# Two changes to a fused attention and expert kernel: three 32-row copies for four 19-row copies, and two key units scored later

## The chip, the cores and the metric

The kernel runs on one core of a Trainium2 chip. The metric is the device time of one execution in microseconds (us); lower is better. Times before: a median of 1031.72 us of three runs (1028.29 to 1032.41).

## The reference

Agent attention over four batches, then a mixture of experts in which each token takes its best expert. Cut to what matters:

```python
B, N, C = 4, 11456, 128;  n_agents = 49;  E, F = 8, 1024
a2k = softmax(scale * agents @ k.T)            # 49 x N per batch
agent_v = a2k @ v                              # 49 x C
q2a = softmax(scale * q @ agents.T)            # N x 49
x = q2a @ agent_v                              # N x C, all tokens 45824 x C
e_idx = argmax(x @ w_gate)
probs, eom = softmax(x @ w_gate), sigmoid(x @ w_output_gate)
h = relu(x @ w1[e]);  out = probs[e] * eom[e] * (h @ w2[e])     # e = e_idx of the token
```

Everything is float32; the kernel splits most factors into a high and a low half in float16.

## The kernel before, in words

Tokens are cut per batch into 12 units: 11 of 1024 tokens (128 partitions by 8) and one of 192 (96 by 2). Each unit of queries gives two tiles of the main products (512 tokens, or one tile of 192), 92 tiles in all.

*Why x need not be formed.* A token's hidden value is relu(e @ (agent_v @ w1)), with e the 49 exponentials of the token. `fold(b)` therefore takes the average values of a batch, picks the one expert that most of its tokens are expected to take (`ei`), loads that expert's `w1t` and `w2t`, and multiplies the first with agent_v (`products`, results `aw`). `first` makes the float16 weights `w` of it. Each half of the 1024 hidden values needs two `w`: one (`rest`) with low parts for the rest of the agents, repeated in four groups of rows, and one (`own_`) of 128 rows: the 49 high weights, the same 49 for the low half of e, and 30 low weights for the high half of e. The 30 low rows and the 19 of `rest` together are all 49 agents. Tokens whose expert is another one are done apart at the end ("left" tiles).

*Turned queries.* `q_rest` makes for each query unit the exponentials `ef`, their high and low half in `e16` (49 + 49 columns, and 30 columns of the high half again, 128 in all), and turns `e16` by a DMA transpose into `x1` (128 rows of 1024 float16 values). Four copies from `x1` into the row groups of a second tile, `x2`, follow; each waits for the transpose. Both tiles are called `x_ld` in the profile. Then the logits (`lg`) are taken from `x1`, and the expert of each token, its factor `smt`, and what the left tiles need (`efd`) follow.

*Main products.* `mm1` multiplies four blocks of `own_` with `x1` and four blocks of `rest` with the four row groups of `x2`, into four PSUM banks (`h`). ACT makes `hh` of it (relu, float16), DVE `hl` (what is left of it), and `mm2` multiplies both with the second weights `vv` into `y`.

*Order.* All instructions are emitted by one program that plays a schedule with its own estimates: `Clock` holds for each engine and tile when it thinks it is free or ready. `main_stream` emits `mm1` and `mm2` when their operands are ready by these estimates; between them `tick` lets other streams go on. While nothing is ready before the main products begin, `idle` emits `warm` products of constants. `clk.started` becomes true with the first `mm1`. Every engine executes in order.

One stream, `small_products`, scores keys, queries and values in the order of `ITEMS`: 12 key units of batch 0, two query units, 12 value units, six key units of batch 1 (`PRE = 6`), then query units mixed with the keys and values of the next batch. A query unit waits until it is at most `AHEAD = 5` units ahead of the main products. `scores` has two forms for whole float32 units: before the start single products of 64 columns each, after it a block of products of 32 columns (`blocked`). `loads` loads the units in the same order; the first `FIRST_ITEMS = 2 * NU + 6` (30) at once, the rest after the weights that `fold` picks. In a unit's float32 products each matmul shows as two records.

All DMAs named here are issued by SP, whose queue is in order too. In the profile nearly all instructions have line L212, that of the helper that emits them, so groups are told apart by their tiles.

Of the kernel before, what the change touches and what calls it, by code (L numbers as in the profile page):

```python
# [17 lines left out]
P = 128  # L18
B, N, C, A, E, F = 4, 11456, 128, 49, 8, 1024
# [14 lines left out]
AD = P - 2 * A  # L34
AR = A - AD
G4 = 4
# [225 lines left out]
def agent_attention_top1_moe(ctx, tc, qT, kT, v, aT, wg, wo, w1, w2, cst, out):  # L262
    nc = tc.nc
    clk = Clock()
    ACT, DVE, POOL = Engine(clk, "ACT", nc.scalar), Engine(clk, "DVE", nc.vector), Engine(clk, "POOL", nc.gpsimd)
    PE, SY = Engine(clk, "PE", nc.tensor), Engine(clk, "SP", nc.sync)
# [42 lines left out]
    def release(k):  # L309
        banks[k][0] = True  # L310
# [143 lines left out]
    halves = {}  # L454
# [119 lines left out]
    parts = {}  # L574
# [44 lines left out]
    def loads():  # L619
        for n, item in enumerate(ITEMS):  # L620
            while n >= FIRST_ITEMS and (picking[0] or len(X1) < 2):
                yield None
# [6 lines left out]
    def scores(item, name):  # L629

        kind, b, u = item
        base, pp, nt = UNITS[u]
        whole = item in WHOLE
        while item not in (parts if whole else halves):
            yield None
        yield from wait_free(True)
        if whole:
            x, inv = parts.pop(item), None
            todo = [(x, at)]
        else:  # L640
            xh, xl, inv = halves.pop(item)
            todo = [(xh, ah), (xh, al), (xl, ah)]
        s = bank(name)
        mark = hold(True)
        if whole and clk.started:
            yield from blocked(s, [(t, x[:, t * pp:(t + 1) * pp], at[:, b, :]) for t in range(nt)])
            scored(item)
            return s, mark, inv
        for t in range(nt):
            if whole and pp == P:  # L650

                for h in range(0, P, 64):
                    yield from PE.q.matmul(s[h:h + 64, t * A2:(t + 1) * A2], x[:, t * pp + h:t * pp + h + 64],
                                           at[:, b, :], start=True, stop=True)
                continue
            for k, (x, a) in enumerate(todo):
                yield from PE.q.matmul(s[0:pp, t * A2:(t + 1) * A2], x[:, t * pp:(t + 1) * pp], a[:, b, :],
                                       start=(k == 0), stop=(k == len(todo) - 1))
        scored(item)
        if not whole:  # L660
            scored_n[0] += 1
        return s, mark, inv

    NU = len(UNITS)
# [162 lines left out]
    def fold(b):  # L827

        ad, ar = avd[b % 2]
        while "rec" not in K[b]:  # L830
            yield None
        av = K[b]["av"]
        yield from DVE.q.tensor_tensor(ad[:, 0:A], av[:, 0:A], K[b]["rec"][:, 0:A], op=ALU.mult)
        if b == 0:
            release(K[0]["mark"])
        sa = wk.tile([P, 1], F32, name=f"sa{b}", tag="sa")
        yield from DVE.q.tensor_reduce(sa, ad[:, 0:A], axis=AX.X, op=ALU.add)
        wgs = wk.tile([P, E], F32, name=f"wgs{b}", tag="wgs")
        yield from DVE.q.tensor_scalar(wgs, wgo[:, 0:E], sa, None, op0=ALU.mult)
        yield from wait_free()  # L840
        ga = bank(f"ga{b}")
        mark = hold()
        yield from PE.q.matmul(ga[:, 0:E], ones, wgs, start=True, stop=True)
        yield from ACT.q.copy(ad[:, A:2 * A], ad[:, 0:A])
        yield from ACT.q.copy(ad[:, 2 * A:P], ad[:, 0:AD])
        yield from POOL.q.tensor_copy(ar[:, :, 0:AR], ad[:, AD:A].unsqueeze(1).broadcast_to([P, G4, AR]))
        gm1 = wk.tile([P, 2], F32, name=f"gm1{b}", tag="gm1")
        yield from DVE.q.tensor_reduce(gm1[:, 0:1], ga[:, 0:E], axis=AX.X, op=ALU.max)
        r1 = wk.tile([P, E], F32, name=f"r1{b}", tag="r1")
        yield from DVE.q.scalar_tensor_tensor(r1, ga[:, 0:E], gm1[:, 0:1], rank8, op0=ALU.is_ge, op1=ALU.mult)  # L850
        release(mark)
        yield from DVE.q.tensor_reduce(gm1[:, 1:2], r1, axis=AX.X, op=ALU.max)
        ei = wk.tile([P, 1], I32, name=f"ei{b}", tag="ei")
        yield from DVE.q.tensor_scalar(ei, gm1[:, 1:2], -1.0, float(E), op0=ALU.mult, op1=ALU.add)
        picking[0] = True
        state[b] = dict(w=[], vv=[])
        spawn(gates(b, ad), -1)
        yield from SY.wait(ei)
        er = nc.values_load(ei[0:1, 0:1], engines=[SP], min_val=0, max_val=E - 1,
                            skip_runtime_bounds_check_because="eight minus a rank of one to eight")  # L860
        w1t = wk.tile([P, F], F32, name=f"w1t{b}", tag="w1t", bufs=2)
        for hf in range(2):
            sl = slice(hf * 512, (hf + 1) * 512)
            yield from SY.q.dma_start(w1t[:, sl], w1[bass.ds(er, 1), :, sl].rearrange("a p f -> p (a f)"))
        w2t = wk.tile([P, F], F32, name=f"w2t{b}", tag="w2t", bufs=2)
        yield from SY.q.dma_start(w2t, w2[bass.ds(er, 1)].rearrange("a p f -> p (a f)"))
        spawn(picked(w2t), -1)
        aw, marks = [], []
        spawn(products(b, ad, ar, w1t, aw, marks), -1)
        ndom = wk.tile([P, E], F32, name=f"ndom{b}", tag="ndom")  # L870
        yield from DVE.q.tensor_scalar(ndom, rank8, gm1[:, 1:2], None, op0=ALU.not_equal)
        state[b]["ndom"] = ndom
        sq = wk.tile([P, 2], F32, name=f"sq{b}", tag="sq")
        for hf in range(2):
            x = wk.tile([P, 512], F16, name=f"wsq{b}_{hf}", tag="whi", bufs=2)
            yield from ACT.q.activation(x, w1t[:, hf * 512:(hf + 1) * 512], AF.Square, accum_out=sq[:, hf:hf + 1])
        while "an" not in state[b]:
            yield None
        r, mark = yield from total(sq, f"mw{b}")
        c1 = wk.tile([P, 1], F32, name=f"c1{b}", tag="c3")  # L880
        yield from DVE.q.tensor_scalar(c1, r, state[b]["an"], None, op0=ALU.mult)
        release(mark)
        s1, s1i = yield from scale(c1, f"s1{b}", 10)
        state[b]["s1i"] = s1i
        spawn(first(b, aw, marks, s1), -1)
        spawn(second(b, w2t), -1)

        yield from wait_free()
        t = bank(f"avn{b}")
        mark = hold()  # L890
        yield from PE.q.transpose(t[0:A, 0:P], ad[:, 0:A], idf)
        avn = wk.tile([P, C], F32, name=f"avn_sb{b}", tag="avn", bufs=1)
        yield from ACT.q.copy(avn[0:A], t[0:A, 0:P])
        release(mark)
        yield from SY.q.dma_start(avnd[b], avn[0:A])
# [120 lines left out]
    def q_rest(b, u, s, mark, inv):  # L1016
        base, pp, nt = UNITS[u]
# [12 lines left out]
        ev = ef[0:pp, 0:nt, 0:A]  # L1030
        yield from ACT.q.activation(ev, z[0:pp, 0:nt, 0:A], AF.Exp,
                                    scale=SCALE if inv is None else inv[0:pp])
        e16 = e16s[(NU * b + u) % 4]
        yield from ACT.q.copy(e16[0:pp, 0:nt, 0:A], ev)
        yield from LOW.q.tensor_tensor(e16[0:pp, 0:nt, A:2 * A], ev, e16[0:pp, 0:nt, 0:A], op=ALU.subtract)
        yield from POOL.q.tensor_copy(e16[0:pp, 0:nt, 2 * A:P], ev[:, :, 0:AD])
        while me > 0 and rests[me - 1] < 1:
            yield None
        while vacant_turned() is None:
# [1 line left out]
        x1 = place(("x1", b, u), vacant_turned()[1], [1024], F16)  # L1041
# [2 lines left out]
        while vacant_turned() is None:  # L1044
            yield None
        x2 = place(("x2", b, u), vacant_turned()[1], [1024], F16)
        for g in range(G4):
            yield from SY.q.dma_start(x2[32 * g:32 * g + AR, 0:nt * pp], x1[AD:A, 0:nt * pp])
        X1[b, u] = x1, x2
        rests[me] = 1  # L1050
        while not {"gs", "ndom"} <= state.get(b, {}).keys() or (me > 0 and rests[me - 1] < 2):
# [110 lines left out]
    MIX = [(3, 0)] * 4 + [(0, 0)] + [(0, 2)] * 6 + [(0, 0)]  # L1162
    ITEMS = order()
    UNIT = {"q": q_unit, "k": k_unit, "v": v_unit}
    FIRST_ITEMS = 2 * NU + 6

    WHOLE = {x for x in ITEMS if x[0] == "k" or x[1] == 0 and x[2] < 8 or x[1] == B - 1}

# [19 lines left out]
    def mm1(i, hf):  # L1188

        b, u, h, pp, n = tiles[i]  # L1190
        w = pp * n
        own_, rest = state[b]["w"][hf]
        x1, x2 = (x[:, 512 * h:512 * h + w] for x in X1[b, u])
        p = []
        for g in range(G4):
            p.append((bank(f"h{i}_{hf}_{g}", k=g), hold()))
            PE.matmul(p[g][0][:, 0:w], own_[:, g * P:(g + 1) * P], x1, start=True, stop=False)
            if g < G4 - 1:
                tick()
        for g in range(G4):  # L1200
            rows = slice(32 * g, 32 * g + AR)
            PE.matmul(p[g][0][:, 0:w], rest[rows, g * P:(g + 1) * P], x2[rows, :], start=False, stop=True)
        for g in range(G4):
            spawn(relu(i, G4 * hf + g, *p[g]), 0)
        tick(0)
        block()
        if hf == 1 and 4 * h + n == UNITS[u][2]:
            for x in ("x1", "x2"):
                scored((x, b, u))
        tick(0)  # L1210
# [546 lines left out]
```

## Time and profile before

| | |
|---|---|
| median of three runs | 1031.72 us (1028.29 to 1032.41) |
| the profiled execution | 1036.13 us |
| its span, first to last instruction | 1034.4 us |
| PE, PEld busy | 971.5 us (94%), 738.6 us (71%) |
| DVE, ACT, POOL busy | 803.7 us (78%), 669.6 us (65%), 429.6 us (42%) |
| mean granted TensorE clock | 0.983 |
| DMA | 146.68 MB, mean 142 GB/s |
| copies from x1 to x2 (`x_ld<-x_ld`) | 192, 38.0 KB each (7.1 KB for the small units) |
| transposes (`x_ld<-e`) | 48 |

A row of a timeline has the start in us, the duration in us, the engine, the line, the operation with what it writes and reads, how many instructions are merged in it, and in brackets how long the engine was idle before it and what ended that. SPq is SP's queue. A row of the waits has the total in us, how many times, and the longest. A row of stretches has, for each engine (PE, PEld, DVE, ACT, POOL), busy us and instructions, then the granted clock, the busy share of the DMA engines and GB/s.

### The profile page before, as it was taken

Reading aid. Unit: us, or ns where it says so; the run is one execution under the profiler, and the core shown is the slowest. Engines: PE = TensorE matmul, PEld = TensorE weight load, DVE = VectorE, ACT = ScalarE, POOL = GpSimd, SP = SyncE. Lnnn points to the kernel's source line nnn. Section 1 sums busy time; section 2 is a strip of 40 time slices with the busy share of each in tenths; the row PEclk is TensorE's granted clock in tenths of the full one; section 3 lists DMA queues with packets and bytes.
Section 4 is the critical chain, followed back from the end, with each engine's and each line's share of the span. In section 5 each row is a group of like instructions: output and inputs, shape, how many; then the busy total and the mean of one; then the engine's idle time right before and its main releaser. Section 6 shows DMA issues by size and latency. Waiting matters only on the chain. (4 is left out here: it accounts for less than half of the span.)

```text
span 1034.4 us, 36058 instructions
## 1 busy us (share of the span) xinstructions
PE 971.5 (94%) x14800; PEld 738.6 (71%) x14800; DVE 803.7 (78%) x2167; ACT 669.6 (65%) x1523; POOL 429.6 (42%) x722
## 2 busy tenths in 40 slices
PE   9879988999999899999999999999998999999985
PEld 8666666777687677776677677776765777888764
DVE  2738877878888778888988878888997876766662
ACT  3336856787778787778688886657554665555542
POOL 1403445564244476453345556522243354442121
PEclk9989999999999999999999999999999999999998
DMA  8975745653556746545377454444342344545020
GB/s 317 273 241 153 149 106 102 160 156 113 169 150 195 159 110 123 160 129 177 93 184 192 124 153 139 144 127 126 97 94 80 107 157 132 153 150 151 23 76 27
DMA packets 106396, 146.68 MB, mean 142 GB/s; under 512 B 60466, under 2 KB 69094, under 8 KB 106228
## 3 DMA queue, kind: packets, MB, share of 16 engines
q1 hardware_dynamic: 104884, 142.86, 49.7%
q8 instruction: 117, 1.92, 0.8%
q0 software_dynamic: 1344, 1.49, 0.7%
q14 instruction: 51, 0.42, 0.1%
HBM read 90.88 MB, written 35.17 MB: 122 GB/s over the span
## 5 line engine op out<-in xcount | busy, mean ns | idle before, releaser
L212 PE MATMUL y<-vv,hh 128*128 128x256 f16 (+1 forms) x2880 | 546.6, 275 | 16.4 <-DVE os L212 7.3
L212 DVE SCALAR_TENSOR_TENSOR hl<-h,hh 128x512 f16<-128x512 f32 (+1 forms) x736 | 448.8, 667 | 92.0 <-ACT hh L212 86.3
L212 PE MATMUL y<-vv,hl 128*128 128x128 f16 (+1 forms) x2880 | 513.5, 220 | 4.7 <-DVE hl L212 3.8
L212 ACT ACTIVATE hh<-h 128x512 f16<-128x512 f32 (+1 forms) x736 | 373.4, 592 | 196.0 <-PE h L212 194.1
L212 PEld LDWEIGHTS <-hh 128*128 128x128 f16 (+1 forms) x2880 | 284.2, 99 | 57.4 <-issue 22.3
L212 PEld LDWEIGHTS <-hl 128*128 128x128 f16 (+1 forms) x2880 | 285.1, 100 | 25.0 <-issue 14.7
L212 PE MATMUL h<-x_ld,w 128*128 128x512 f16 (+1 forms) x1472 | 260.8, 377 | 4.6 <-DVE hl L212 4.0
L212 PEld LDWEIGHTS <-w 128*128 128x128 f16 x1472 | 83.1, 94 | 108.5 <-issue 77.0
L212 POOL TENSOR_TENSOR os<-os,smt 128x512 f32<-128x512 f32 (+1 forms) x92 | 96.2, 1046 | 117.3 <-DVE os L212 94.6
L212 DVE TENSOR_TENSOR os<-y,ys 128x256 f32<-128x256 f32 x180 | 74.9, 416 | 42.6 <-ACT ys L212 39.9
L212 ACT COPY ys<-y 128x256 f32<-128x256 f32 x180 | 68.6, 381 | 53.0 <-PE y L212 47.7
L212 POOL TENSOR_TENSOR e<-ef,e 128x392 f16<-128x392 f32 (+1 forms) x48 | 42.3, 881 | 63.5 <-ACT e L212 63.4
L212 POOL TENSOR_TENSOR q_ld<-q_ld,xhq 128x1024 f16<-128x1024 f32 (+1 forms) x28 | 55.0, 1965 | 28.0 <-ACT q_ld L212 27.5
L212 POOL TENSOR_TENSOR ev<-S,km_o 128x400 f32<-128x400 f32 (+1 forms) x44 | 42.2, 961 | 42.1 <-PE av L212 38.0
L212 PE MATMUL ks<-at,k_ld 128*32 128x50 f32 (+1 forms) x2280 | 48.9, 216 | 7.9 <-DMA k_ld<-kT 5.7
L212 PEld LDWEIGHTS ks<-at,k_ld 128*32 128x32 f32 (+1 forms) x2280 | 41.9, 119 | 17.8 <-issue 14.7
L212 PE MATMUL lh<-lxs,lw_ld 128*128 128x128 f32 x224 | 43.4, 275 | 0.8 <-ACT lxs L212 0.8
L212 PE MATMUL ly<-lw_ld,lh 128*128 128x128 f32 x224 | 43.2, 275 | 0.0
L212 PEld LDWEIGHTS <-xhq 128*128 128x128 f16 (+1 forms) x412 | 33.5, 97 | 10.3 <-issue 4.1
L212 PE MATMUL lg<-gs,x_ld 128*128 128x36 f16 x360 | 33.9, 181 | 6.1 <-DMA x_ld<-e 4.9
L212 POOL TENSOR_TENSOR ll<-lL,rr 128x128 f32<-128x128 f32 (+1 forms) x48 | 19.1, 398 | 48.8 <-DVE rr L212 46.9
L212 PEld LDWEIGHTS <-x_ld 128*128 128x128 f16 x360 | 27.2, 99 | 16.3 <-DMA x_ld<-e 7.2
(273 smaller groups left out, 1313.7 us busy)
## 6 DMA issues: line engine op xcount, KB each, us to landing
q_ld<-qT SPq DMA_DIRECT2D x44, 512.0 KB
v_ld<-v SPq DMA_DIRECT2D x44, 512.0 KB
out<-os SPq DMA_DIRECT2D x88, 256.0 KB
k_ld<-kT SPq DMA_DIRECT2D x43, 512.0 KB
lw_ld<-w SPq DMA_DIRECT2D x28, 512.0 KB
efd<-ef SPq DMA_DIRECT2D x44, 200.0 KB
x_ld<-x_ld SPq DMA_DIRECT2D x176, 38.0 KB
w1t<-w SPq DMA_DIRECT2D x8, 256.0 KB
```

Of the source, the lines that this page charges most:

```text
L212: return getattr(self.eng, op)(*a, **k)
```

## The change

The 30 agents whose low weights stand in the 128-row product are now the last 30 instead of the first 30, and the 19 in groups the first 19. Rows 0 to 18 of `x1` are these 19 agents, and they already lie where group 0 reads them. So group 0 reads `x1` itself, and three copies fill the groups 1 to 3 of `x2`; each takes 32 rows of `x1` instead of 19. Apart from that, the key units 4 and 5 of batch 1 wait in `scores` until the main products have begun, and with them all that follows them in `small_products`. `FIRST_ITEMS` is written in another way and keeps its value, 30.

```diff
@@ scores
-        while item not in (parts if whole else halves):
+        while item not in (parts if whole else halves) or kind == "k" and b == 1 and u >= EARLY and not clk.started:
             yield None
@@ fold
         yield from ACT.q.copy(ad[:, A:2 * A], ad[:, 0:A])
-        yield from ACT.q.copy(ad[:, 2 * A:P], ad[:, 0:AD])
-        yield from POOL.q.tensor_copy(ar[:, :, 0:AR], ad[:, AD:A].unsqueeze(1).broadcast_to([P, G4, AR]))
+        yield from ACT.q.copy(ad[:, 2 * A:P], ad[:, AR:A])
+        yield from POOL.q.tensor_copy(ar[:, :, 0:AR], ad[:, 0:AR].unsqueeze(1).broadcast_to([P, G4, AR]))
@@ q_rest
-        yield from POOL.q.tensor_copy(e16[0:pp, 0:nt, 2 * A:P], ev[:, :, 0:AD])
+        yield from POOL.q.tensor_copy(e16[0:pp, 0:nt, 2 * A:P], ev[:, :, AR:A])
...
-        for g in range(G4):
-            yield from SY.q.dma_start(x2[32 * g:32 * g + AR, 0:nt * pp], x1[AD:A, 0:nt * pp])
+        for g in range(1, G4):
+            yield from SY.q.dma_start(x2[32 * g:32 * g + 32, 0:nt * pp], x1[0:32, 0:nt * pp])
@@
-    FIRST_ITEMS = 2 * NU + 6
+    EARLY = 4
+    FIRST_ITEMS = 2 * NU + 2 + EARLY
@@ mm1
-            PE.matmul(p[g][0][:, 0:w], rest[rows, g * P:(g + 1) * P], x2[rows, :], start=False, stop=True)
+            PE.matmul(p[g][0][:, 0:w], rest[rows, g * P:(g + 1) * P], (x2 if g else x1)[rows, :], start=False, stop=True)
```

With A = 49, P = 128: AD = 30, AR = 19, G4 = 4, NU = 12.

## The prediction

> **What bounds the kernel now.** I read first the page's busy times, then the stretches, to see where TensorE stands still, then its waits, then the timeline around the largest one.
>
> ```profile
> PE 971.5 (94%) x14800; PEld 738.6 (71%) x14800; DVE 803.7 (78%) x2167; ACT 669.6 (65%) x1523; POOL 429.6 (42%) x722
> ```
>
> ```profile
> 50.00:75.00 25.00, 18.84 (x261) 14.23 (x260) 8.54 (x32) 7.19 (x19) 0.62 (x3) 0.84 0.69 226
> 75.00:100.00 25.00, 24.65 (x498) 17.89 (x496) 20.81 (x59) 16.42 (x40) 6.75 (x17) 0.95 0.52 146
> ...
> 125.00:150.00 25.00, 21.04 (x259) 14.73 (x258) 20.02 (x54) 14.18 (x33) 12.53 (x20) 0.93 0.58 134
> ```
>
> ```profile
> PE y L212 <- DVE os L212: 7.3, 6, 2.0
> PE ks L212 <- DMA k_ld<-kT: 5.7, 1, 5.7
> PE lg L212 <- DMA x_ld<-e: 4.9, 3, 2.7
> ```
>
> TensorE is busy for 94% of the span; the next engine, DVE, for 78%. So an end moves if TensorE's idle time or its work moves. The stretches (columns: PE, PEld, DVE, ACT, POOL busy, granted clock, DMA share, GB/s) show two holes that the change can reach: 6.16 us of idle PE in 50 to 75 and 3.96 us in 125 to 150, both with a clock below 1. The waits name them: one of 5.7 us for a load of keys, three of together 4.9 us for turned queries. Both are waits for DMA.
>
> The first hole, on PE, ACT, DVE and the queue of SP:
>
> ```profile
> 63.68 1.45 PE L212 MATMUL aw<-w1t,avd 128*128 128x512 f32 x3
> 70.86 0.85 PE L212 MATMUL ks<-at,k_ld 128*64 128x50 f32 x10 [5.72 <-DMA k_ld<-kT]
> 71.64 0.45 PE L212 MATMUL avn<-kc,avd 128*49 128x128 f32 x1
> 72.02 1.52 PE L212 MATMUL ks<-at,k_ld 128*64 128x50 f32 x22
> ```
>
> ```profile
> 73.80 1.96 PE L212 MATMUL ks<-at,k_ld 128*64 128x50 f32 x32
> ```
>
> ```profile
> 76.01 1.89 PE L212 MATMUL qs<-at,q_ld 128*64 128x50 f32 x32
> 77.83 0.94 PE L212 MATMUL warm<-idle_x 128*128 128x256 f16 x7
> 78.70 0.44 PE L212 MATMUL ks<-at,k_ld 128*64 128x50 f32 x8
> 79.07 1.04 PE L212 MATMUL h<-x_ld,w 128*128 128x512 f16 x4
> ```
>
> ```profile
> 64.35 0.69 ACT L212 ACTIVATE whi<-aw,s_s 128x512 f16<-128x512 f32 x1 [1.55 <-DVE s1d L212]
> 72.12 0.26 ACT L212 COPY avn_sb<-avn 49x128 f32<-49x128 f32 x1 [7.09 <-PE avn L212]
> 72.28 0.68 ACT L212 ACTIVATE whi<-aw,s1d 128x512 f16<-128x512 f32 x1
> ```
>
> ```profile
> 74.69 1.41 DVE L212 SCALAR_TENSOR_TENSOR w<-aw,s_s,whi 128x512 f16<-128x512 f32 x2
> ```
>
> ```profile
> 55.39 0.92 SPq L212 DMA_DIRECT2D w1t<-w  x2
> 56.93 0.33 SPq L212 DMA_DIRECT2D w2t<-w  x1
> 57.37 2.76 SPq L212 DMA_DIRECT2D x_ld<-x_ld  x4
> 60.24 0.89 SPq L212 DMA_DIRECT2D k_ld<-kT  x2
> ```
>
> FIRST_ITEMS admits 30 items before the picked weights: 12 key, 2 query and 12 value units of batch 0, and key units 0 to 3 of batch 1. So the first load of keys behind the weights, at 60.24, is k(1,4). Its 32 score records are the ten at 70.86 and the 22 at 72.02; the 32 at 73.80 are k(1,5), and at 76.01 comes q(0,2). These are the two key units of the change and the query unit behind them in the same stream. TensorE's queue is in order: it stood before k(1,4) from 65.13 (63.68 + 1.45) to 70.86. Behind it stood the small product avn at 71.64; behind its copy, ACT's in-order queue stood from 65.04 to 72.12; and behind that the second to fourth parts of the first weights w, the last of them done at 76.10 (74.69 + 1.41). The main products (h) can't begin before these, and begin at 79.07. So one late load holds up the whole start.
>
> Why was the load late? It was issued at 60.24, behind the four copies x2 at 57.37, and let TensorE go 10.6 us later. Bandwidth doesn't explain that: from 55.39 on, w1t, w2t, the four copies and k(1,4) are by their shapes 512 + 512 + 152 + 512 KB, 1.73 MB, which at 226 GB/s of that stretch take 7.7 us, so until 63.1; it came 7.8 us later. The same is seen in steady state:
>
> ```profile
> 128.23 2.46 SPq L212 DMA_DIRECT2D x_ld<-x_ld  x4
> 130.80 1.50 SPq L212 DMA_TRANSPOSE x_ld<-e  x1
> ```
>
> ```profile
> 138.40 0.22 PE L212 MATMUL lg<-gs,x_ld 128*128 128x36 f16 x2 [2.72 <-DMA x_ld<-e]
> ```
>
> ```profile
> 788.05 1.28 SPq L212 DMA_TRANSPOSE x_ld<-e  x1
> ```
>
> ```profile
> 791.62 2.46 SPq L212 DMA_DIRECT2D x_ld<-x_ld  x4
> ```
>
> A transpose right behind four copies is waited for until 138.40, 7.6 us after its issue. One with no copies ahead had landed 3.6 us after its issue, since the copies of 791.62 read it. The copies hold up what follows them by about 4 us, far more than their bytes would.
>
> **The change part by part.** (1) *Copies.* Per unit four copies of 19 rows become three of 32; group 0 reads the turned tile itself. Matmul shapes, the two ACT copies and the POOL copies keep their sizes (30 and 19 columns), so TensorE, ACT, DVE and POOL get nothing more or less. On SP:
>
> ```profile
> L212 SPq DMA_DIRECT2D x_ld<-x_ld x192: 561/562/1072, 42.8 to 931.3; - x192
> ```
>
> ```profile
> L212 SPq DMA_DIRECT2D k_ld<-kT x25: 327/328/597, 1.5 to 85.4; - x25
> ```
>
> An issue of 19 rows takes 0.562 us of SP, a load of 128 rows 0.328. For 32 rows I bound the issue by 0.328 and by 0.562 x 32/19 = 0.947: 1.0 to 2.8 us per unit in place of 2.25. Nothing of it counts: no wait of TensorE in the trace names SP, and if they became longer, the next to be late would be the transposes, whose delay is priced next. The bytes grow from 76 to 96 rows of 2 KB per unit, 40 KB, or 0.18 us at 226 GB/s.
>
> What counts is how long the copies hold up what follows. From above: as long as now. From below: not at all, so that a transpose lands in 3.6 us in place of 7.6. The longest of the three waits for x_ld (2.7) is shorter than these 4.0 us, so all 4.9 us can go. I take 3.5, nearer to the lower bound, because 0.18 us of bytes can't explain a hold of 4 us, so what the copies cost is in the shape of 19 rows; I leave 1.4 because a PE that waits no more for x_ld meets the next wait of the same place (DVE is busy for 20.02 of these 25 us). Ends kept: 0 and 4.9. Of the clock of 0.93 in that stretch (0.07 x 25 = 1.75 us of work) I take 0.5 back; ends 0 and 1.75.
>
> The rule that bears on this: the Trainium skill, "DMA: Bandwidth & Descriptors", section "Why a DMA increments its semaphore by 16 and not by 1", says that a copy from SP runs on the largest number of DMA engines up to 16 that divides its row count. By that rule 19 rows run on one engine and 32 on 16, and the trace agrees as far as the 7.6 against 3.6 us go, though no view here shows single DMA engines. By the rule the whole 4.9 us would go and the sum below would be 11.8 in place of 10.4.
>
> (2) *Key units.* The load order doesn't change: FIRST_ITEMS is 30 in both. k(1,4), k(1,5) and all behind them in the stream (q(0,2), half of k(1,6)) are now scored once the main products have begun. The stall would go by either part alone; here both act, so it is counted once. What is left of the start: aw ends at 65.13, then avn (0.45) and its copy (0.26): the second whi starts at about 65.85 in place of 72.28. From there the last w ended 3.82 us later (76.10) and h began 6.79 us later (79.07), behind q(0,2), warming products and ks. Bounds for the new start of h: 65.85 + 3.82 = 69.7 and 65.85 + 6.79 = 72.6. Without scores in the way only the 0.94 us of warming products stand after the last w; the mx of 0.58 us goes. I take 70.0, near the lower end: 9.1 us earlier (ends 6.5 and 9.4).
>
> Against this stands the work that now comes after the start, on a TensorE without idle time (24.65 of 25 us busy in 75 to 100):
>
> ```profile
> 84.39 0.92 PE L212 MATMUL qs<-at,q_ld 128*32 128x50 f32 x64
> ```
>
> ```profile
> 93.58 0.91 PE L212 MATMUL ks<-at,k_ld 128*32 128x50 f32 x64
> ```
>
> In the form used after the start two key units cost 2 x 0.91 and q(0,2) 0.92: 2.7 us. Net 6.4 us; ends 3.8 and 6.7. On ACT and DVE the same units bring about 2 us each (two S copies and maxima of 0.5 to 0.6, and two passes for the queries); they lie in DVE's 4.2 and ACT's 8.6 idle us of 75 to 100. If that cover is gone, hl comes late, and TensorE with it.
>
> (3) *The planner.* It prices three copies in place of four and shifts every later choice a little. I take 0; ends plus and minus 7.3, the largest group of waits above, since a reordering can lose or gain one such group.
>
> Sum: 6.4 + 3.5 + 0.5 = 10.4 us. The profiled execution took 1036.13, so 1025.7 for it; it lies 4.4 above the median of the three runs, 1031.72, so I predict 1031.72 - 10.4 = 1021.3. From here on 0.5% (5.2 us) is about what a measurement of this kernel can tell from no change.
>
> **The rivals.**
>
> *Given back.* The stream begins the main products three units further behind. If q(0,2)'s turned rows are late for tile 4, the net 6.4 us of the start are lost there.
>
> ```profile
> L212 PE MATMUL h<-x_ld,w x1472: 242/379/605, 79.1 to 1016.6; 128*128 128x512 f16 x176, 128*128 128x192 f16 x8
> ```
>
> ```profile
> 85.96 2.39 SPq L212 DMA_TRANSPOSE x_ld<-e  x1
> ```
>
> ```profile
> 95.00 2.46 SPq L212 DMA_DIRECT2D x_ld<-x_ld  x4
> ```
>
> 92 tiles in 937.5 us are 10.2 us per tile, so tile 4 comes 41 us after the start. Before, q(0,2) was scored at 76.01, its transpose went out 10 us and its copies 19 us later, and a hold of some 8 as above may lie behind them; scored about 6 us after the start it is ready at 33 at the latest. For: a DVE busy for 20.81 of 25 us. Against: 8 us of slack. It decides when the rows come over 8 us later than reckoned. Then 3.5 + 0.5 = 4.0 remain: 1027.7, no change.
>
> *Slower: batch 1's weights late.* They need all keys of batch 1, so two late key units lie on their chain.
>
> ```profile
> 288.75 0.74 DVE L212 SCALAR_TENSOR_TENSOR w<-aw,s_s,whi 128x512 f16<-128x512 f32 x1
> ```
>
> ```profile
> 306.63 2.06 ACT L212 ACTIVATE hh<-h 128x512 f16<-128x512 f32 x4 [0.49 <-PE h L212]
> ```
>
> The last w of batch 1 ends at 289.5, its first tile's h is taken up at 306.6: 17 us of slack. If the stream stays behind and each of the two units costs a whole query unit (two tiles, 20.4 us), the weights come 40.8 us late, and 24 us of stall against 10.4 gained give 1045. It decides from 17 us of lateness. Against: queries are held to five units ahead of the main products, so the stream waits there and catches up.
>
> *More than reckoned.* If the copies hold up every load on its way, part of the waits under other names go too: the 7.3 us for os, whose stores leave through the same DMAs, and the last 1.4 of the x_ld. 10.4 + 7.3 + 1.4 = 19.1: 1012.6. For: out stores are issued amid the copies. Against: those waits name DVE. By the skill's rule named above, one engine would carry all 192 copies, which speaks for this one.
>
> *The copies do not get faster.* A 32-row copy costs 32/19 of one of 19 rows, three in place of four: 26% more hold. Then the waits of 4.9 us grow by 1.3 and nothing comes back: 6.4 - 1.3 = 5.1: 1026.6.
>
> **How the numbers follow.** Forecast 0.62, given back 0.20, weights late 0.06, more than reckoned 0.07, copies not faster 0.05. The forecast's own range goes by the ends of terms (1) and (2): 6.7 + 4.9 + 1.75 = 13.4 gives 1018, 3.8 gives 1028. The range adds the given-back case, a reordering on top of it, and most of the way to the best case: 1013 to 1030, which leaves out the weights and part of the best. Faster by over 0.5% (under 1026.6): the forecast but for 0.02 at its upper end, the best case and half of the last, 0.70; slower: the weights, and 0.01 for a reordering that costs more than all that is gained, 0.07; no change 0.23.
>
> **What would show it.** Right: no wait of ks for k_ld near 65, h beginning near 70, a clock near 1.00 in 50 to 100, no second whi long behind the first, 144 copies and no wait of lg for x_ld. Wrong in (1): a transpose behind copies still taking over 7 us. Wrong in (2): h after 73, or a TensorE wait between 100 and 120 for x_ld. Wrong in (3): new waits of several us for DVE in places where there were none. The stretch from first to last h, 937.5 us, should change by 2.7 - 4.0, to about 936; if it grows by 5 or more, the gain was given back.

## The result, and the profile after

The changed kernel takes 999.77 us (median of four runs, 998.12 to 1004.34) against 1030.01 us for the kernel before (four runs): a ratio of 0.971, interval 0.967 to 0.976. That is 30 us, three times the 10.4 us that were predicted, and below the stated range. The profiled execution took 1001.17 us, 35.0 less than that of before; the profiled execution of before, 1036.13 us, was slower than any of the four runs, so the two profiles differ by some 5 us more than the runs do. First the busy times and the three stretches that the prediction began with:

```profile
span 999.1 us, 36275 instructions
...
PE 959.9 (96%) x14940; PEld 732.2 (73%) x14940; DVE 804.2 (80%) x2167; ACT 669.2 (67%) x1523; POOL 432.0 (43%) x722
```

```profile
50.00:75.00 25.00, 22.71 (x435) 16.94 (x432) 13.63 (x46) 12.03 (x29) 2.59 (x8) 0.97 0.72 246
75.00:100.00 25.00, 23.77 (x502) 16.68 (x504) 21.83 (x52) 15.21 (x36) 5.74 (x12) 1.00 0.53 148
...
125.00:150.00 25.00, 24.61 (x329) 18.45 (x327) 23.09 (x61) 16.86 (x42) 13.68 (x24) 1.00 0.58 147
```

Of the first hole 2.3 of 6.2 us of idle time are left, of the second 0.4 of 4.0. Of the 35.3 us of span, TensorE's idle time gives 23.7 (span less busy: 62.9 before, 39.2 after). The other 11.6 are TensorE's busy time, 971.5 to 959.9, with more matmul records than before, at a higher granted clock (0.983 to 0.994 in the mean).

TensorE's timeline at the start, where the load of k(1,4) had held it:

```profile
65.60 0.27 PE L212 MATMUL avn<-kc,avd 128*49 128x128 f32 x1
65.71 0.49 PE L212 MATMUL warm<-idle_x 128*128 128x256 f16 x3
66.72 2.02 PE L212 MATMUL warm<-idle_x 128*128 128x256 f16 x17 [0.52 <-ACT avn_sb L212]
68.57 0.81 PE L212 MATMUL h<-x_ld,w 128*128 128x512 f16 x3
69.60 0.70 PE L212 MATMUL h<-x_ld,w 128*128 128x512 f16 x5 [0.21 <-DVE w L212]
70.23 0.92 PE L212 MATMUL ks<-at,k_ld 128*32 128x50 f32 x64
```

The main products begin at 68.57 instead of 79.07, and the key units follow in the form that costs 0.92 us each. TensorE's waits, where those of 5.7 us for `k_ld` and 4.9 us for `x_ld` stood:

```profile
PE y L212 <- DVE os L212: 3.2, 3, 1.5
PE y L212 <- ACT S L212: 2.4, 5, 0.7
...
PE lg L212 <- DMA x_ld<-e: 0.2, 1, 0.2
```

How far ahead the changed kernel is when a tile's first `hh` starts (worked out from the starts of ACT's `hh` rows, eight to a tile; us before less us after):

| tile | 0 | 5 | 6 | 12 | 24 | 28 | 64 | 68 | 76 | 84 | 91 |
|---|---|---|---|---|---|---|---|---|---|---|---|
| ahead by | 10.1 | 6.1 | 10.4 | 15.7 | 14.3 | 18.3 | 20.6 | 21.4 | 29.1 | 36.1 | 35.2 |

So the start went as predicted: 6.1 us net at tile 5 against 6.4 reckoned. The stretch behind it, tiles 5 to 12, brought 9.6 against 4.0 reckoned. And two gains were not in the prediction at all: 4 us near tile 27 (where TensorE had stood still for 2.2 us at 342.77, for no wait that the profile shows) and 14 us in the last batch, from tile 68 on. The same three parts in stretches, first of before, then of after (columns as before: PE, PEld, DVE, ACT, POOL, clock, DMA share, GB/s):

```profile
100.00:200.00 100.00, 90.38 (x1467) 66.73 (x1465) 82.84 (x213) 68.85 (x154) 48.45 (x84) 0.98 0.62 135
200.00:700.00 500.00, 484.36 (x8320) 363.92 (x8319) 423.74 (x1126) 379.75 (x838) 247.48 (x412) 1.00 0.54 146
700.00:980.00 280.00, 269.28 (x3150) 208.28 (x3150) 217.14 (x631) 161.65 (x388) 101.62 (x169) 0.99 0.41 117
```

```profile
100.00:200.00 100.00, 98.26 (x1719) 73.25 (x1707) 86.13 (x226) 76.34 (x169) 54.73 (x88) 1.00 0.55 149
200.00:700.00 500.00, 486.48 (x8275) 364.46 (x8273) 434.57 (x1159) 385.05 (x853) 246.26 (x416) 1.00 0.57 151
700.00:980.00 280.00, 277.22 (x3229) 217.28 (x3227) 219.34 (x633) 161.90 (x390) 104.41 (x166) 1.00 0.40 115
```

TensorE's idle time falls by 7.9 us in 100 to 200 and by 7.9 in 700 to 980, and hardly between. In the last batch no wait of before names a DMA. From 720 us on the waits were

```profile
PE y L212 <- DVE hl L212: 3.8, 4, 1.2
PE qs L212 <- issue: 3.6, 8, 0.8
PE h L212 <- DVE hl L212: 2.9, 5, 2.0
```

and in the kernel after, from 700 us on,

```profile
PE y L212 <- DVE hl L212: 1.1, 3, 0.5
PE lg L212 <- DVE os L212: 0.7, 1, 0.7
```

Two theories offered themselves. *S, the shape of the copies:* all that is gained comes from transfers that are no longer held up. *O, the order:* the planner, told of other copies and of waiting key units, laid out the instructions in another order, which happens to have fewer holes. They can be told apart here, because the order is made by the planner's estimates alone: a kernel can be given the real transfers of one kind and the planned ones of another, and then every engine has the same instructions in the same order.

### The profile page after: what moved, and what is told of

Read it like the earlier page. It is cut to its first block, busy times and chain, and to the rows that moved or that the text cites. A ratio compares the mean times of both kernels' runs of the same rounds, so it can differ in the third digit from the quotient of the medians.

```text
span 999.1 us, 36275 instructions
## 1 busy us (share of the span) xinstructions
PE 959.9 (96%) x14940; PEld 732.2 (73%) x14940; DVE 804.2 (80%) x2167; ACT 669.2 (67%) x1523; POOL 432.0 (43%) x722
## 5 line engine op out<-in xcount | busy, mean ns | idle before, releaser
L212 PE MATMUL y<-vv,hh 128*128 128x256 f16 (+1 forms) x2880 | 539.4, 273 | 13.8 <-DVE os L212 3.2
L212 POOL TENSOR_TENSOR q_ld<-q_ld,xhq 128x1024 f16<-128x1024 f32 (+1 forms) x28 | 55.0, 1964 | 24.6 <-ACT q_ld L212 24.5
L212 PE MATMUL ks<-at,k_ld 128*32 128x50 f32 (+1 forms) x2376 | 45.7, 212 | 0.0
L212 PEld LDWEIGHTS ks<-at,k_ld 128*32 128x32 f32 (+1 forms) x2376 | 39.1, 115 | 8.5 <-issue 5.6
L212 PE MATMUL qs<-al,xhq 128*128 128x50 f16 (+1 forms) x206 | 37.8, 184 | 0.0
L212 PE MATMUL qs<-ah,q_ld 128*128 128x50 f16 (+1 forms) x206 | 37.8, 184 | 0.0
```

The source lines that it names most:

```text
L212: return getattr(self.eng, op)(*a, **k)
```

## Experiments

Each ratio is to the kernel before, run on the same chip.

**Copies alone.**

```diff
-        while item not in (parts if whole else halves) or kind == "k" and b == 1 and u >= EARLY and not clk.started:
+        while item not in (parts if whole else halves):
```

> The three 32-row copies alone; key units 4 and 5 of batch 1 are scored early as before. The prediction's parts count about 10 us for the whole change, the chip gave 30. Theory S (the shape of the copies: a copy of 19 rows moves on a narrow path that holds up all other transfers behind it, key loads, transposes, perhaps instruction fetches too): nearly the whole gain is here, the key load is there in time without any waiting of the key units; 1000 to 1006 us, no PE wait for k_ld near 65. Theory O (the order: the waiting key units make the planner lay out everything after the start in another order that happens to have fewer holes): only the stall for k_ld and the waits for turned rows go, about 10 us: 1018 to 1024 us.

1006.78 us, ratio 0.973 (0.970 to 0.976), just above the 1000 to 1006 of Theory S. Nearly the whole gain is here, and no wait for `k_ld` is left, though k(1,4) is scored early. But this kernel also has a new order, so it does not part S from O by itself.

**Waiting key units alone**, on the kernel before:

```diff
-        while item not in (parts if whole else halves):
+        while item not in (parts if whole else halves) or kind == "k" and b == 1 and u >= 4 and not clk.started:
```

> The kernel before with the waiting of key units 4 and 5 alone; the four 19-row copies stay. Theory S: only the start moves, by the 6.4 us net that the prediction reckoned, and the holes after it stay: 1021 to 1026 us. Theory O: most of the gain is here: 1000 to 1010 us. In both h begins near 69 to 70.

1021.74 us, ratio 0.987 (0.984 to 0.990), 14 us. h began at 69.58, and at tile 4 the kernel was 7.1 us ahead, as Theory S had it. It is then 12.8 ahead at tile 12 and ends 14.4 ahead. In 100 to 200 TensorE is idle for 4.9 us in this order against 9.6 before; the waits of lg for x_ld are 1.5 us of that (3.4 against 4.9), and what removed the rest is not shown.

**31 rows, the order of the changed kernel.** The planner is told of 32 rows, the copy takes 31:

```diff
-            yield from SY.q.dma_start(x2[32 * g:32 * g + 32, 0:nt * pp], x1[0:32, 0:nt * pp])
+            o_, i_ = x2[32 * g:32 * g + 32, 0:nt * pp], x1[0:32, 0:nt * pp]
+            yield "SP", [i_], [o_], 1
+            SY.emit("dma_start", [i_], [o_], (x2[32 * g:32 * g + 31, 0:nt * pp], x1[0:31, 0:nt * pp]), {})
```

> The changed kernel with every instruction of every engine in its order; only each copy takes 31 rows of x1 instead of 32 (the rows 19 to 31 of a group are never read, so nothing of the computation changes). 3% fewer bytes. Theory S: 31 rows are, like 19, not spread; 93 rows per unit in one row of transfers against 76 before, so the holes come back: 1020 to 1030 us, with waits of lg for x_ld in 125 to 175 again. Theory O: 998 to 1002 us, like the changed kernel. The Trainium skill, DMA: Bandwidth & Descriptors, section Why a DMA increments its semaphore by 16 and not by 1, has 31 rows on one DMA engine and 32 on 16; that is Theory S in its strongest form.

1046.49 us, ratio 1.014 (1.008 to 1.020): one row less, and the kernel is some 4% slower than the changed one and slower than the kernel before. That is the direction of Theory S, and more than the 1020 to 1030 us that it gave. Its waits of TensorE:

```profile
PE lg L212 <- DMA x_ld<-e: 22.7, 9, 5.8
PE xrq L212 <- ACT xhq L212: 3.9, 2, 2.2
```

The second row is probably the same hold at one remove: ACT's `xhq` waits for a query load, for 2.1 us in the kernel before, for none in the changed kernel, and here for 6.7:

```profile
ACT xhq L212 <- DMA q_ld<-qT: 6.7, 3, 3.1
```

**The old order with the new copies.** The kernel before, its planner told of four 19-row copies; three 32-row copies are issued, and the layout is that of the change (the part of the edit in `q_rest`):

```diff
-            yield from SY.q.dma_start(x2[32 * g:32 * g + AR, 0:nt * pp], x1[AD:A, 0:nt * pp])
+            o_, i_ = x2[32 * g:32 * g + AR, 0:nt * pp], x1[AD:A, 0:nt * pp]
+            yield "SP", [i_], [o_], 1
+            real = (x2[32 * g:32 * g + 32, 0:nt * pp], x1[0:32, 0:nt * pp]) if g else None
+            SY.emit("dma_start", [i_], [o_], real, {})      # None: nothing is issued
```

> The kernel before with every instruction of every engine in its order, early key units included, but with the data layout and the three 32-row copies of the change in place of the four 19-row ones (the planner is told the old four). Theory S: the copies alone, without any other order, bring nearly all: 1000 to 1008 us. Theory O: 1018 to 1028 us.

1016.49 us, ratio 0.981 (0.978 to 0.985): 19 us, between the two theories. The shape of the copies is worth 19 us by itself, and the rest of the gain, some 10 us, is not the transfers. TensorE at the start of this kernel:

```profile
65.45 0.55 PE L212 MATMUL ks<-at,k_ld 128*64 128x50 f32 x10
65.93 0.31 PE L212 MATMUL avn<-kc,avd 128*49 128x128 f32 x1
66.17 0.90 PE L212 MATMUL ks<-at,k_ld 128*64 128x50 f32 x22
67.22 1.14 PE L212 MATMUL ks<-at,k_ld 128*64 128x50 f32 x32
...
70.82 1.36 PE L212 MATMUL h<-x_ld,w 128*128 128x512 f16 x8
```

k(1,4) is scored without a wait, and h begins at 70.82, though all key units stand before it. The kernel is 8.3 us ahead at tile 0, 15.2 at tile 12 and 16.3 at the end (of the profiled execution, 1019.78 us). It keeps the holes of the last batch:

```profile
PE qs L212 <- issue: 3.9, 9, 0.5
PE y L212 <- DVE hl L212: 2.9, 3, 1.2
PE h L212 <- DVE hl L212: 2.5, 5, 1.7
```

**20 rows and 19 rows, the order of the changed kernel.** The edit is that of 31 rows with another number.

> The changed kernel with its order, each of the three copies taking 20 rows instead of 32. So far: 32 rows 0.971 of the kernel before, 31 rows in the same order 1.014. Theory E (one engine): a copy is spread over the largest number up to 16 that divides its rows, so 20 rows go over ten, two each, as quickly as 32 over 16: ratio 0.966 to 0.976, no wait of lg for x_ld over 1 us in all. Rival T (only full rows of 16 or the partition boundary matter, or the number of bytes): 20 rows are no multiple of 16 and behave like 19 and 31: ratio 0.99 to 1.01.

> The same with 19 rows: one row less than the kernel before it, 57 rows per unit on one path by Theory E against 93 with 31 rows and 76 before. By the 31-row run, 93 rows cost 0.043; in proportion 57 rows cost at most 0.026, less if short holds hide: ratio 0.976 to 0.998, with some wait of lg for x_ld. If 19 and 20 rows take the same time, Theory E falls.

20 rows: 1000.93 us (999.89 to 1003.32), ratio 0.968 (0.962 to 0.974), no wait for x_ld. 19 rows: 1007.29 us (1006.13 to 1011.03), ratio 0.974 (0.968 to 0.981), and

```profile
PE lg L212 <- DMA x_ld<-e: 2.9, 2, 2.4
```

The intervals of the two ratios overlap, but no run of the one reaches the other's. The ratio of 19 rows lies just under what was expected. Theory E stands and Rival T falls: 20 is no multiple of 16, and is as quick as 32. This is the rule of the Trainium skill that the prediction named ("DMA: Bandwidth & Descriptors", section "Why a DMA increments its semaphore by 16 and not by 1"): 19 and 31 rows on one DMA engine, 20 on ten, 32 on 16. The traces' single DMA packets agree: in the profile before, 76 packets of 2048 bytes, four copies of 19 rows, follow one another from 61.29 to 68.74 us, each beginning as the one ahead of it ends (they overlap by at most 0.02 us). That is the hold that kept k(1,4) from landing. The same can be counted wherever the packets of one unit's copies stand apart from others of their size:

| rows | units | packets in each | us from first to last | at most at once |
|---|---|---|---|---|
| 4 x 19 (before) | 8 | 76 | 6.1 to 7.4 | 1 |
| 3 x 19 | 6 | 57 | 4.6 to 6.1 | 1 |
| 3 x 31 | 3 | 93 | 7.8 to 9.0 | 1 |
| 3 x 20 | 10 | 60 | 1.0 to 2.2 | 10 |
| 3 x 32 (changed) | 8 | 96 | 1.1 to 3.8 | 16 |

The packets also tell when a transpose of 1024 tokens had landed, counted from its issue (medians):

| kernel | with copies issued in the 9 us ahead | with none |
|---|---|---|
| before, 4 x 19 rows | 5.4 us | 3.7 us |
| changed order, 3 x 31 | 7.1 | 4.0 |
| changed order, 3 x 19 | 4.6 | 3.9 |
| changed order, 3 x 20 | 3.8 | 4.0 |
| changed, 3 x 32 | 3.8 | 4.3 |

The price isn't in proportion: in the order of the changed kernel 57 rows one after another cost 6 us of kernel time over 20-row copies, 93 rows some 45. That short holds hide in the lead that the planner gives to transfers is likely, but no run shows it.

**Both parts at the old price.** The kernel of the old order with new copies, and the waiting key units:

> Both parts of the change, the planner told the old four 19-row copies: the instruction order of the gate-only kernel (0.987), with the 32-row copies. It differs from the changed kernel only in the price that the planner sets on the copies. Theory S+O (the copies' shape removes waits, about 0.019 in the old order, and the new price happens to give an order with 0.009 fewer holes): gate only has fewer lg waits (3.4 us against 4.9) so the shape brings 0.008 to 0.015 here: ratio 0.972 to 0.979, slower than the changed kernel. If the waiting key units themselves add their 6.4 us to the old-order copies (0.981): 0.975.

1015.50 us, ratio 0.982 (0.976 to 0.988), more than the 0.972 to 0.979 that were expected and the same as without the waiting (0.981). At the new price it is the same: 0.971 with, 0.973 without. So beside quick copies the waiting is worth nothing that can be measured: it brings h from 70.82 to 68.57 and pays the 2.7 us of scores afterwards. Alone it had avoided the same late load.

**Copies alone, priced as 19 rows; and three issues priced as dear as the old four.** The part of both edits in `q_rest`; the key units don't wait:

```diff
-            yield from SY.q.dma_start(x2[32 * g:32 * g + 32, 0:nt * pp], x1[0:32, 0:nt * pp])
+            o_, i_ = x2[32 * g:32 * g + AR, 0:nt * pp], x1[0:AR, 0:nt * pp]      # dear: 25 for AR
+            yield "SP", [i_], [o_], 1
+            SY.cost = lambda *a: 640.0                                           # dear alone
+            SY.emit("dma_start", [i_], [o_], (x2[32 * g:32 * g + 32, 0:nt * pp], x1[0:32, 0:nt * pp]), {})
```

> Copies alone, three issues of 32 rows, each priced by the planner as 19 rows. A third order with the same transfers: old order with new copies gave 0.981, copies-only with the true price 0.973. If the planner's price were itself of use (it tells when x2 lands), this would lie between; if the order is a lottery, anywhere from 0.968 to 0.986, and its holes after 700 us decide: about 9 us of idle PE there as in the old order, or about 2.5.

> Copies alone, three issues of 32 rows, but priced by the planner so that in all they take as long as the four old ones: 640 ns of SP each (3 x 640 = 4 x 480) and the bytes of 25 rows. Old price (two kernels): 0.981 and 0.982; new price (three kernels): 0.970 to 0.973. Theory P (the time of SP that the planner reckons for the copies picks the order, the number of issues does not): 0.978 to 0.985, with holes of together 7 us or more after 720 us. Theory N (the number of issues): 0.968 to 0.975. Theory L (any change of any estimate gives an order of its own, with no rule in it): anywhere from 0.965 to 0.99.

0.970 (0.964 to 0.976) and 0.968 (0.965 to 0.972). The first does not lie between 0.973 and 0.981, as it would if the true price were of use to the planner. The second was to show that the reckoned time of SP decides, at 0.978 to 0.985, and did not: Theory P fell. Its order is another one again (engine by engine, the instructions of the two traces differ in some 3,300 lines from the old order and in some 3,900 from that of copies alone, buffer numbers left out), and it has only 5 us of idle TensorE after 720 us.

**A candidate, and two draws.** Both parts, 20 rows, priced as 19; then one unrelated estimate of the planner changed in both orders with 32-row copies:

```diff
-LANDS = 1500.0
+LANDS = 1300.0
```

> A candidate: both parts of the change, 20 rows copied instead of 32 (20 rows in place of 32 took 0.968 against 0.971) and priced as 19 rows (0.970 against 0.973 without waiting key units). If these three small gains add: 0.964; if they are noise of the measurement: 0.967 to 0.974.

> The old order with 32-row copies (0.981), with one estimate of the planner changed that has nothing to do with the copies: it allows 1300 instead of 1500 ns for a transfer to land. Theory L: a fresh draw, 0.968 to 0.988. Theory P (the old price itself is what makes the holes of the last batch): 0.977 to 0.985.

> Copies alone at their own price (0.973), with the same change from 1500 to 1300 ns. Theory L: a fresh draw, 0.966 to 0.988. Theory P: 0.968 to 0.976, without the holes after 720 us.

The candidate took 1008.38 us, 0.973 (0.969 to 0.977): small gains of single edits do not add. The old order moved to 1011.03 us, 0.976 (0.972 to 0.979), and the new one to 1016.60 us, 0.981 (0.977 to 0.985). An estimate that has nothing to do with the copies moves the time by 5 and by 9 us, and turns the two orders round. Theory L holds, and with the new order at 0.981 Theory N, that three issues make the quick order, falls as well. All kernels whose copies are quick, with TensorE's idle time from their profiles (gaps between matmuls):

| kernel | ratio | idle 60 to 720 | idle after 720 |
|---|---|---|---|
| changed | 0.971 | 18.3 us | 2.8 us |
| the same order, 20 rows | 0.968 | 18.0 | 3.7 |
| three dear | 0.968 | 18.6 | 5.3 |
| priced as 19 | 0.970 | 20.4 | 3.8 |
| copies alone | 0.973 | 20.8 | 4.3 |
| candidate | 0.973 | 22.7 | 4.6 |
| old order, LANDS 1300 | 0.976 | 22.9 | 5.7 |
| new order, LANDS 1300 | 0.981 | 24.5 | 9.3 |
| old order | 0.981 | 20.7 | 11.1 |
| old price, waiting units | 0.982 | 19.7 | 10.0 |
| for comparison: before | 1 | 32.8 | 12.0 |

None of them beats the changed kernel by more than the measurement can tell. Nine orders, quick copies in all of them, 0.968 to 0.982.

## Why the prediction was wrong, point by point

*What bounds the kernel.* Right. The gain is TensorE's idle time and its clock; DVE, now at 80%, did not take over.

*The cause of the late load.* Right, and shown: with the old order and quick copies the wait is gone. Most of the 10.6 us of k(1,4) were the packets of the copies ahead of it, which ended at 68.85.

*(2), the key units: 9.1 less 2.7.* The net was right (6.1 at tile 5 for 6.4), and partly by luck: h came 10.5 us earlier, beyond the upper end of 9.4, and 4.4 of it were gone by tile 5 in place of 2.7. That the stall is counted once because either part removes it was right too: 0.987 for the one, 0.981 for the other, and with quick copies the waiting adds nothing.

*(1), the copies: 3.5 + 0.5.* The mechanism was right, the term too small. Tiles 5 to 12 brought 9.6 us. The old order with quick copies shows this term by itself, since there only the transfers differ from the kernel before. It is 8.6 us ahead at tile 5 and 15.2 at tile 12, so the term is 6.7:

```profile
100.00:200.00 100.00, 95.36 (x1558) 71.30 (x1557) 85.90 (x226) 75.25 (x168) 56.52 (x95) 1.00 0.55 147
```

TensorE is idle for 4.6 us there in place of 9.6, which is 5.0 us and all that the waits for `x_ld` (4.9) could give, and the clock is back at 1.00, worth 1.7. These are the upper ends that I had stated, 4.9 and 1.75. The step that failed is what I took off: I left 1.4 us to the next wait of the same place, which took nothing (the waits for `os` in this stretch are 2.0 us in both kernels), and I gave the clock 0.5. The other 2.9 of the 9.6 us are the order: the changed kernel is idle for 1.7 us in this stretch.

*The clock* was too small everywhere. In all 14 profiles of this study it stands at 1.00 or, for 3.4 us or a multiple of that, at 0.50 (but for the last stretch, which the end cuts off). In the kernel before, TensorE was busy for 23.7 us at 0.50, in the changed kernel for 3.4. At full clock half of each would have done, by estimate, so 10.2 of the 11.6 us are the clock's. Behind the first 60 us and ahead of the end it fell five times in the kernel before, at 67.5, 139.1, 343.9, 797.9 and 989.1 us, and never in the changed one. Each time TensorE had been busy for less than half of the 3.4 us ahead, as here at the wait for `x_ld`:

```profile
135.70:139.11 3.41, 0.71 (x9) 0.44 (x9) 1.53 (x5) 0.00 (x0) 2.80 (x6) 1.00 0.40 125
139.12:142.53 3.41, 3.41 (x25) 2.14 (x23) 1.69 (x4) 2.47 (x6) 0.13 (x1) 0.50 0.22 78
142.54:146.00 3.46, 3.46 (x74) 2.46 (x76) 2.99 (x10) 1.39 (x4) 1.86 (x4) 1.00 0.30 94
```

In the 14 profiles no fall from 1.00 after the first 60 us follows such a stretch that was busier than 0.57, though not every idle one is followed by a fall. So one hole of 2 to 3 us cost up to 1.7 us more (half of 3.4), and the many small ones nothing. In the first hole it lasted for three times 3.4 us; its row shows 0.50 as well:

```profile
69.00:72.00 3.00, 1.14 (x11) 0.87 (x11) 0.00 (x0) 0.00 (x0) 0.00 (x0) 0.50 0.97 381
```

The Trainium skill, "TensorE: Matmul & The Clock Gate", section "Part 1: The HAM clock gate", says that the clock passes either all pulses or half of them by how busy TensorE has lately been; the 0.50 agrees.

*(3), the planner: 0.* This is the larger miss, a term put at nothing because its sign was not known. The order that the new price gave is worth about 10 us (0.981 to 0.973 without the waiting units, 0.982 to 0.971 with them), nearly all in the last batch, where 11.1 and 10.0 us of idle time after 720 us became 4.3 and 2.8, and where 10.2 us at half clock, in the profiles of both old orders, became none. That it came out as a gain was luck, as the draws show. The stated ends of plus and minus 7.3 us were right as a spread, since nine orders lie within 14 us of one another. But I set the range as if only one term would err: its lower end, 1013, lies 8.3 under the forecast, little more than this one term, and (1) and its clock were short in the same direction. The sum in the prediction's own terms: in the old order the transfers alone brought 19 us where all terms together were 10.4, and the new order brought some 10 where the term was 0.

*The rivals.* "More than reckoned" (0.07) came nearest, at 1012.6, with the right mechanism and with another source for most of the size: the waits for os did fall, from 7.3 to 3.2, but with the old order and quick copies they stayed at 7.3. So they were the order's, not the copies'. "Given back", "weights late" and "copies not faster" did not happen. The stretch from first to last h is 912.7 us (68.6 to 981.3), where 936 was reckoned.

*SP's issue* of a 32-row copy took 0.582 us, between the bounds of 0.328 and 0.947, and was hidden, as said.

*Open.* Why the queries' scores of the last batch stutter at "issue" (3.9 us in nine waits in the old order with quick copies, none in the changed kernel, 1.3 in three in the same order with 19, 20 or 31 rows) no run shows. It goes more with the order than with the copies. What TensorE stood still for at 342.77 in the kernel before, no run shows either. Why one order has fewer holes than another was not traced further.

## What to carry to other kernels

Read the row counts of all small copies: here those of 19 and 31 rows moved one packet at a time and held up what was issued behind them, and those of 20 and 32 rows did not; the remedy, a few rows more that no one reads, cost 0.02 us of issue. When a late transfer stalls TensorE, price the whole wait that names it, and add the clock: here up to 1.7 us for each hole that left TensorE idle for more than about half of 3.4 us. Where a planner makes the order, a change of its estimates is a draw of its own: here 14 us between the best and the worst, more than many edits are worth, so keep the order fixed to measure an edit, and draw orders on purpose afterwards.

## What the hardware showed that was not expected

How sharp the step is: 20 rows took 1000.93 us and 19 rows 1007.29, 32 rows 0.971 and 31 rows 1.014 of the kernel before. The issue on SP doesn't follow the row count either: 0.562 us for 19 and for 31 rows, 0.707 for 20 and 0.582 for 32 (medians).

```profile
L212 SPq DMA_DIRECT2D x_ld<-x_ld x144: 706/707/1757, 42.1 to 897.5; - x144
```

```profile
L212 SPq DMA_DIRECT2D x_ld<-x_ld x144: 512/582/1942, 43.2 to 898.5; - x144
```

The first row is of 20 rows, the second of 32.
